# VectorE's selection of the second half of a slot's activations is placed behind the sum of snap and pz

## The chip, the cores and the metric

The kernel runs on one core of one Trainium2 chip. A core has five engines with an instruction stream each: TensorE (PE in the profile, with its weight loads as PEld), VectorE (DVE), ScalarE (ACT), GpSimd (POOL) and SyncE (SP). An engine works through its stream in order, and the engines wait for each other by semaphores. The metric is the device time of one execution in microseconds (us); the kernel before takes 1406.0 us (median of 3 runs, 1404.99 to 1407.55).

## The reference

Three stages follow each other, all in float32, on 8 batches of 512 tokens and 32 states:

```python
# attention both ways between x (8, 8, 512, 64) and state (8, 8, 32, 64)
a  = softmax(scale * x @ state.T);   xread = a @ state
a2 = softmax(scale * state @ x.T);   sread = a2 @ x
x = concat([xread, sread])           # 8 * (512 + 32) = 4352 tokens of 512
# first stage of products
x = ((x @ w_a) * (x @ w_b)) @ w_out          # w_a, w_b 512 x 1536
# second stage of products
h = x @ w_in                                  # w_in 512 x 2048
out = (h - tanh(h)) @ w_out2                  # w_out2 2048 x 512
```

The weights arrive as 64-bit numbers; the kernel decodes them on the chip.

## The kernel before

The attention and the first stage of products fill roughly the first half of the time. The second stage is what the change touches. Its work is cut into slots: 9 blocks of tokens (8 of 512, the last, the states, of 256) times 8 slots `j`. A slot computes two of the sixteen 128-row blocks of `h`, `h1` and `h2`, applies `h - tanh(h)` to them and multiplies by two 128-row pieces of the last weight matrix. A slot's own products are written by `pair_slot` (L777) as seven sums of 6 matmuls each of 128x256 (`part`, L690; a fixed 2x2 scheme with 7 products instead of 8), into three PSUM banks `py`, `px` and `pz`. Every float32 product is three matmuls of high and low halves. `px` is summed up over four parts and read in between: ScalarE copies it to `snap` (L787, L798, L813) and, the last time, into `h1` (L822). `pz` takes the parts T3 and T4: VectorE adds `snap` and `pz` into the right half of `h2` after T3 (L814, `at_v`) and into the left half after T4 (L830). T4 is added into the same bank that L814 reads, so T4 waits for L814. `h1` and `h2` have one buffer each.

The activation of the slot before runs meanwhile, in two halves g = 0 (on `h1`) and g = 1 (on `h2`), with work tiles u, t, y, k:

- ScalarE: u = h squared (L700), t = tanh h (L703), y = (u + c) squared (L711), k = relu(u - 0.49) (L715), which says where |h| is large.
- VectorE: `dve_yu` computes y (L719) and u (L720), `dve_rest` finishes the polynomial in y (L724), forms t = h - t (L725) and selects t into y where k is set (L726, the selection).
- ScalarE copies y to the high half of g (`g_hi`, L730), VectorE subtracts it for the low half (`g_lo`, L735).

`O(s, g, m)` (L747) multiplies g by the last weights into the accumulators `acc`: 6 matmuls of 128x256 for each of 4 accumulators `m`, of which the first two read the high half alone. In `pair_slot(s)` the O of slot s-2 with g = 1 and of slot s-1 with g = 0 stand between the parts. Of the 90 matmuls of a slot 42 are parts and 48 are O.

In steady state TensorE's order in a slot is: py 6, px 6, O 12 (s-2), px T2 6, pz T3 6, O 6, px T1 6, O 6 (the last of s-2) and O 6 (the first of s-1), px B22 6, O 6, pz T4 6, O 12.

The weights `wh` of a slot are loaded from DRAM by two DMAs (L272) into the buffers of slot s-2, the first with the pieces of the parts py, px, T2 and T3, the second with those of T1, B22 and T4.

What order an engine's stream has is decided when the program is built: a scheduler walks over the instructions with an estimate of their times and places what is ready first. `tc.issue_after(x)` adds an edge of order: what is written in its block comes behind x on x's engine. The edge has no semaphore of its own.

Of the kernel before, what the change touches and what calls it, by code (L numbers as in the profile page):

```python
# [12 lines left out]
ALU = mybir.AluOpType  # L13
# [32 lines left out]
def fused_kernel(ctx: ExitStack, tc, xT, xn, stp, stq, wA, wB, outT, outS):  # L46
    nc = tc.nc
# [592 lines left out]
    GG, HH, EW, RAWX = {}, {}, {}, {}  # L640
# [26 lines left out]
    def x_split(blk, i):  # L667
        b11, b12, b21, b22 = x_blocks(blk)
        if blk == NB:
            if i < 2:  # L670
                x_pair(blk, ("B11", "B21")[i], i, (b11, b21)[i])
        else:
            name, at, src = (("B11", 0, b11), ("B22", 2, b22), ("B21", 1, b21), ("T1", 3, b12), ("T2", 4, b22),
                             ("T3", 5, b11), ("T4", 6, b21))[i]
            x_pair(blk, name, at, src)

    def x_minus(blk, i):
        b11, b12, b21, b22 = x_blocks(blk)
        if blk < NB and i < 4:
            out, a, b = ((b12, b12, b11), (b22, b22, b12), (b21, b21, b22), (b11, b22, b11))[i]  # L680
            nc.vector.tensor_tensor(out, a, b, ALU.subtract)
# [5 lines left out]
    def part(dst, s, piece, x, first, last):  # L687
        for k in range(2):
            for i, (a, c) in enumerate(hi_lo):
                nc.tensor.matmul(dst, WP[s, piece][:, a, block(k)], XB[slots[s][0]][x][:, c, k, :],  # L690
                                 start=first and k == 0 and i == 0, stop=last and k == 1 and i == 2,
                                 skip_group_check=True)
# [5 lines left out]
    def act_u(s, g):  # L698
        ew_open(s, g)
        nc.scalar.activation(EW[s, g][0], HH[s][g], AF.Square)  # L700

    def act_t(s, g):
        nc.scalar.activation(EW[s, g][1], HH[s][g], AF.Tanh)  # L703

    def act_ut(s, g):
        act_u(s, g)
        act_t(s, g)

    def act_y(s, g):
        u, t, y, k = EW[s, g]  # L710
        return nc.scalar.activation(y, u, AF.Square, bias=consts[:, 0:1], scale=1.0)  # L711

    def act_k(s, g):
        u, t, y, k = EW[s, g]
        nc.scalar.activation(k, u, AF.Relu, bias=const2[:, 0:1], scale=1.0)  # L715

    def dve_yu(s, g):
        u, t, y, k = EW[s, g]
        nc.vector.scalar_tensor_tensor(y, y, PK, u, ALU.add, ALU.mult)  # L719
        nc.vector.scalar_tensor_tensor(u, t, C3, u, ALU.mult, ALU.mult)  # L720

    def dve_rest(s, g):
        u, t, y, k = EW[s, g]
        nc.vector.scalar_tensor_tensor(y, y, PC, u, ALU.add, ALU.mult)  # L724
        nc.vector.tensor_tensor(t, HH[s][g], t, ALU.subtract)  # L725
        nc.vector.copy_predicated(y, k.bitcast(I32), t)  # L726

    def g_hi(s, g):
        GG[s, g] = big.get([128, 2, 512], F32R, "g", MX + PHS + ["w21"])
        nc.scalar.copy(GG[s, g][:, 0, : width(s)], EW[s, g][2])  # L730

    def g_lo(s, g):
        n = width(s)
        gt = GG[s, g]
        return nc.vector.tensor_tensor(gt[:, 1, :n], EW.pop((s, g))[2], gt[:, 0, :n].bitcast(F32), ALU.subtract)  # L735

    def O(s, g, m):
        if not 0 <= s < len(slots):
            return
        (blk, j), n = slots[s], width(s)  # L740
        if j == 0 and g == 0:
            acc[m] = accp.tile([128, 512], F32, tag=f"acc{m}", name="acc")
        w, x = pair(WB[j + FP * g], block(m)), GG[s, g]
        cols = half[: n // 256]
        for i, (a, c) in enumerate(hi_lo):
            for h in cols:
                nc.tensor.matmul(acc[m][:, h], w[a], x[:, c, h], start=j + g + i == 0 and h is half[0],  # L747
                                 stop=j + g == FP and i == 2 and h is cols[-1], skip_group_check=True)

    def evac(s, g, m):  # L750
        if not 0 <= s < len(slots) or slots[s][1] < FP - 1 or g == 0:
            return
        (blk, j), n = slots[s], width(s)
        if m % 2 == 0:
            EV[0] = big.get([128, 2, 512], F32, "ev", RAW)
        e = EV[0][:, m % 2, :n]
        if m % 2 and blk == NB:
            nc.vector.tensor_copy(e, acc[m][:, :n])
        else:
            nc.scalar.copy(e, acc[m][:, :n])  # L760
        nc.sync.dma_start(outT[blk, m] if blk < NB else outS[m], e)
# [3 lines left out]
    def bank(i, name):  # L765

        pool = LAST[0] if i < 2 else abp
        return pool.tile([128, 512], F32, tag=f"p{i}", name=name)[:, half[0]]

    def OE(s, g, m):  # L770
        O(s, g, m)
        evac(s, g, m)

    def pair_slot(s):

        blk, j = slots[s]
        y_ = bank(0, "py")  # L777
        x_ = bank(1 + 2 * (s % 2), "px")
        sn = mix.get([128, 3, 256], F32, "snap", SQ)
        h1, h2 = (mix.get([128, 512], F32, "h", [nm]) for nm in (mix.names[2], "ml2"))  # L780
        part(y_, s, 2, "B21", True, True)
        part(x_, s, 1, "B11", True, True)
        yield
        if s:
            dve_rest(s - 1, 0)
            act_ut(s - 1, 1)
        first = nc.scalar.copy(sn[:, 0], x_)  # L787
        if s:
            with tc.issue_after(first.ins):
                act_y(s - 1, 1)  # L790
                act_k(s - 1, 1)
        OE(s - 2, 1, 0)
        OE(s - 2, 1, 1)
        if s:
            dve_yu(s - 1, 1)
        nc.vector.tensor_tensor(h1[:, half[0]], sn[:, 0], y_, ALU.add)
        part(x_, s, 3, "T2", False, True)
        second = nc.scalar.copy(sn[:, 1], x_)  # L798
        if s:
            with tc.issue_after(second.ins):  # L800
                g_hi(s - 1, 0)
            low = g_lo(s - 1, 0)
            with tc.issue_after(low.ins):
                dve_rest(s - 1, 1)
        z_ = bank(2 if s else 0, "pz")
        part(z_, s, 4, "T3", True, True)
        yield
        OE(s - 2, 1, 2)
        part(x_, s, 5, "T1", False, True)
        yield  # L810
        nxt = border.index(blk) + 1
        stage = j - 1 if j > 1 or blk == 0 else (0, None)[j]
        at_s = nc.scalar.copy(sn[:, 2], x_)  # L813
        at_v = nc.vector.tensor_tensor(h2[:, half[1]], sn[:, 2], z_, ALU.add)  # L814
        OE(s - 2, 1, 3)
        O(s - 1, 0, 0)
        follow = stage not in (None, -1) and nxt < len(border)
        if follow:
            with tc.issue_after(at_s.ins), tc.issue_after(at_v.ins):
                x_split(border[nxt], stage)  # L820
        part(x_, s, 6, "B22", False, True)
        whole = nc.scalar.copy(h1[:, half[1]], x_)  # L822
        if s:
            with tc.issue_after(whole.ins):
                g_hi(s - 1, 1)
            g_lo(s - 1, 1)
        yield
        O(s - 1, 0, 1)
        part(z_, s, 7, "T4", False, True)
        done = nc.vector.tensor_tensor(h2[:, half[0]], sn[:, 1], z_, ALU.add)  # L830
        if follow:
            with tc.issue_after(done.ins):
                x_minus(border[nxt], stage)
        O(s - 1, 0, 2)
        O(s - 1, 0, 3)
        HH[s] = h1, h2
        act_u(s, 0)
        squared = act_y(s, 0)
        with tc.issue_after(squared.ins):
            act_t(s, 0)  # L840
            act_k(s, 0)
        dve_yu(s, 0)
# [12 lines left out]
    def ew_between(s):  # L855
        dve_rest(s, 0)
        act_ut(s, 1)
        act_y(s, 1)
        act_k(s, 1)
        g_hi(s, 0)  # L860
        dve_yu(s, 1)
        g_lo(s, 0)
        dve_rest(s, 1)
        g_hi(s, 1)
        g_lo(s, 1)
# [60 lines left out]
    for blk in range(NB):  # L926
# [7 lines left out]
        for f in range(FA):  # L934
            v, t = stg[f] if stg else (None, None)
# [83 lines left out]
    first_pool.__exit__(None, None, None)  # L1019
    LAST.append(ctx.enter_context(tc.tile_pool(name="lastp", bufs=1, space=psum)))  # L1020
    slot = pair_slot(0)
    for f in range(FA):
        stages = {4: (0,), 5: (1, 2), 6: (3, 4), 7: (5, 6)}.get(f, ())
# [17 lines left out]
    for s, (blk, j) in enumerate(slots):  # L1041
        if s == 0:
            continue
        if j == 0 and blk < NB:
            xr_load(blk + 1)
        if blk < NB:
            for i, _ in enumerate(pair_slot(s)):
                if s == 1 and i == 0:
                    X1(NB, FA - 1)
        else:  # L1050
            plain_slot(s)
        if s < last - 1:
            wh_load(s + 2, slots[s + 2][1], nb=slots[s + 2][0] == NB)
# [53 lines left out]
```

## Time and profile before

| what | value |
|---|---|
| median of 3 runs | 1406.0 us (1404.99 to 1407.55) |
| the profiled execution, whole | 1407.53 us |
| its span, first to last instruction | 1405.7 us |
| PE busy | 1381.0 us, 98% |
| DVE busy | 1127.3 us, 80% |
| ACT busy | 896.3 us, 64% |
| granted TensorE clock, mean | 0.995 |
| second stage in pair slots | about 698 to 1349 us |

The page gives busy time by engine; the timeline gives single instructions, with start and duration, and runs of equal ones merged (xN). A matmul's duration in it overlaps the next one's, so the time that N matmuls take is read from start to start. On VectorE and ScalarE too the next instruction often starts before the end of the one before; what counts for a chain is again start to start, or end to start across engines. An idle time before an instruction stands in brackets with what ended it.

### The profile page before, as it was taken

The numbers are of one execution on the slowest core, as the hardware profiler recorded it, in microseconds if no ns is written. First come the engines' busy times: TensorE is split into PE (matmuls) and PEld (weight loads), VectorE is DVE, ScalarE is ACT, GpSimd is POOL, SyncE is SP. The second block draws the span as 40 slices with busy tenths as digits, with TensorE's granted clock in tenths as the row PEclk, the third lists the DMA queues.
The fourth block names the chain that finished last, engine by engine and source line by source line (L and its number), as shares of the span: only waits on it lengthen the run. The fifth ranks groups of instructions, "written<-read, shape, count | busy, mean of one in ns | idle before, by whom it ended". The sixth has DMA issues, their size and how long they took to land.

```text
span 1405.7 us, 26998 instructions
## 1 busy us (share of the span) xinstructions
PE 1381.0 (98%) x10464; PEld 1243.7 (88%) x10464; DVE 1127.3 (80%) x1972; ACT 896.3 (64%) x1740; POOL 207.4 (15%) x390
## 2 busy tenths in 40 slices
PE   6999999999999999999999999999999999999998
PEld 3667777888888888889999999999999999999998
DVE  7986657786644878772489999999999999998887
ACT  6765545564544556552467878778787877878675
POOL 0000001333111333321210111110111111011110
PEclk8999999999999999999999999999999999999999
DMA  9714457785546586855856757666675766667544
GB/s 382 262 53 148 135 159 233 222 270 163 159 130 194 177 263 217 257 180 170 292 181 201 227 169 231 188 215 210 201 227 168 232 187 218 210 188 221 168 148 132
DMA packets 103792, 280.69 MB, mean 200 GB/s; under 512 B 15216, under 2 KB 44400, under 8 KB 93936
## 3 DMA queue, kind: packets, MB, share of 16 engines
q0 software_dynamic: 41472, 178.28, 41.1%
q1 hardware_dynamic: 62192, 100.68, 22.0%
q8 instruction: 82, 1.34, 0.4%
q14 instruction: 46, 0.38, 0.1%
HBM read 216.53 MB, written 62.39 MB: 198 GB/s over the span
## 4 chain that ended last, share of the span: by engine, by line
PE 89%; DVE 6%; issue 2%; DMA 2%; ACT 1%; POOL 0%; SPq 0%; DVEq 0%; ACTq 0%; POOLq 0%
PE acc L747 26%; PE pab L464 19%; PE acc L464 17%; PE px L690 12%; PE pz L690 6%; PE py L690 3%; PE mq L555 2%; PE ph L851 1%; DMA raw<-in_wA 1%; PE sc L337 1%; DMA wh<-whd 1%; DVE mst L562 1%; DVE wa L133 0%; PE pr L412 0%; PE pt L349 0%
## 5 line engine op out<-in xcount | busy, mean ns | idle before, releaser
L747 PE MATMUL acc<-g,wo 128*128 128x256 f32 x3264 | 427.2, 277 | 0.3
L747 PEld LDWEIGHTS acc<-g,wo 128*128 128x128 f32 x3264 | 397.3, 188 | 1.0 <-DVE g L735 0.8
L464 PE MATMUL acc<-ph,wo 128*128 128x512 f32 (+1 forms) x1296 | 304.2, 380 | 0.0
L464 PE MATMUL pab<-hl,mx 128*128 128x512 f32 x1152 | 289.1, 397 | 2.3 <-DVE mst L562 2.2
L464 PEld LDWEIGHTS acc<-ph,wo 128*128 128x128 f32 x1296 | 230.6, 188 | 48.6 <-issue 3.7
L464 PEld LDWEIGHTS pab<-hl,mx 128*128 128x128 f32 x1152 | 211.3, 189 | 56.4 <-issue 6.8
L602 DVE TENSOR_TENSOR ac<-ac,pab 128x512 f32<-128x512 f32 (+1 forms) x108 | 70.7, 654 | 140.8 <-PE pab L464 140.5
L272 POOL DMA_DIRECT2D wh<-whd x144 | 77.6, 539 | 632.1 <-PE pz L690 581.9
L577 POOL DMA_DIRECT2D ml<-md x144 | 75.6, 527 | 402.8 <-DVE mx L583 235.9
L720 DVE SCALAR_TENSOR_TENSOR u<-t,u 128x512 f32<-128x512 f32 (+1 forms) x144 | 95.0, 660 | 23.2 <-ACT k L715 21.6
L599 ACT COPY ac<-pab 128x512 f32<-128x512 f32 (+1 forms) x108 | 60.5, 560 | 79.9 <-PE pab L464 79.7
L690 PE MATMUL pz<-T,wh 128*128 128x256 f32 x768 | 111.3, 281 | 0.0
L690 PE MATMUL px<-B,wh 128*128 128x256 f32 x768 | 108.7, 277 | 2.3 <-DMA wh<-whd 2.3
L726 DVE COPY_PREDICATED y<-k,t 128x512 f32<-128x512 int32 (+1 forms) x144 | 105.2, 730 | 4.7
L690 PE MATMUL px<-T,wh 128*128 128x256 f32 x768 | 108.2, 277 | 0.0
L735 DVE TENSOR_TENSOR g<-y,g 128x512 fp32r<-128x512 f32 (+1 forms) x144 | 95.1, 660 | 13.5 <-ACT g L730 10.1
L719 DVE SCALAR_TENSOR_TENSOR y<-y,u 128x512 f32<-128x512 f32 (+1 forms) x144 | 94.3, 655 | 10.6 <-ACT y L711 10.6
L711 ACT ACTIVATE y<-u,consts 128x512 f32<-128x512 f32 (+1 forms) x144 | 100.8, 700 | 2.7 <-DVE g L735 0.6
L690 PEld LDWEIGHTS px<-B,wh 128*128 128x128 f32 x768 | 96.9, 188 | 2.7 <-issue 2.5
L715 ACT ACTIVATE k<-u,const 128x512 f32<-128x512 f32 (+1 forms) x144 | 99.0, 687 | 0.0
L690 PEld LDWEIGHTS pz<-T,wh 128*128 128x128 f32 x768 | 97.7, 189 | 0.4 <-DVE h L814 0.2
L724 DVE SCALAR_TENSOR_TENSOR y<-y,u 128x512 f32<-128x512 f32 (+1 forms) x144 | 95.0, 660 | 2.5
(161 smaller groups left out, 2040.2 us busy)
## 6 DMA issues: line engine op xcount, KB each, us to landing
wh<-whd POOLq DMA_DIRECT2D x64, 1024.0 KB, 5.3
wh<-whd POOLq DMA_DIRECT2D x72, 768.0 KB, 4.8
ml<-md POOLq DMA_DIRECT2D x144, 128.0 KB, 2.8
raw<-in_wB SPq DMA_DIRECT2D x32, 512.0 KB, 4.6
whd<-hlb POOLq DMA_DIRECT2D x64, 256.0 KB, 3.1
rawab<-in_wA SPq DMA_DIRECT2D x12, 1024.0 KB, 9.4
md<-mst SPq DMA_DIRECT2D x48, 256.0 KB, 2.6
x1d<-ev SPq DMA_DIRECT2D x32, 256.0 KB, 3.3
```

Of the source, the lines that this page charges most:

```text
L272: nc.gpsimd.dma_start(t.rearrange("p a h c -> p a (h c)"), whd[j][:, a:b])
L464: nc.tensor.matmul(dst[:, cols], w[a], x[:, c, cols], start=first and i == 0, stop=last and i == 2)
L577: nc.gpsimd.dma_start(t[64 * G : 64 * G + 64, :], src[G, b])
L690: nc.tensor.matmul(dst, WP[s, piece][:, a, block(k)], XB[slots[s][0]][x][:, c, k, :], start=first and k == 0 and i == 0, stop=last and k = ...
L711: return nc.scalar.activation(y, u, AF.Square, bias=consts[:, 0:1], scale=1.0)
L715: nc.scalar.activation(k, u, AF.Relu, bias=const2[:, 0:1], scale=1.0)
L719: nc.vector.scalar_tensor_tensor(y, y, PK, u, ALU.add, ALU.mult)
L720: nc.vector.scalar_tensor_tensor(u, t, C3, u, ALU.mult, ALU.mult)
L724: nc.vector.scalar_tensor_tensor(y, y, PC, u, ALU.add, ALU.mult)
L726: nc.vector.copy_predicated(y, k.bitcast(I32), t)
L735: return nc.vector.tensor_tensor(gt[:, 1, :n], EW.pop((s, g))[2], gt[:, 0, :n].bitcast(F32), ALU.subtract)
L747: nc.tensor.matmul(acc[m][:, h], w[a], x[:, c, h], start=j + g + i == 0 and h is half[0], stop=j + g == FP and i == 2 and h is cols[-1], s ...
```

## The change

`dve_rest` is split into `dve_poly` (L724 and L725) and `dve_select` (L726). For the second half (g = 1) of the slot before, `pair_slot` calls `dve_poly` where `dve_rest` stood, and calls `dve_select` later, behind `at_v`, the sum of snap and pz, by an edge of order. The first half and the plain slots of the last block keep `dve_rest`.

```diff
     def dve_rest(s, g):
+        dve_poly(s, g)
+        dve_select(s, g)
+
+    def dve_poly(s, g):
         u, t, y, k = EW[s, g]
         nc.vector.scalar_tensor_tensor(y, y, PC, u, ALU.add, ALU.mult)
-        nc.vector.tensor_tensor(t, HH[s][g], t, ALU.subtract)
+        return nc.vector.tensor_tensor(t, HH[s][g], t, ALU.subtract)
+
+    def dve_select(s, g):
+        u, t, y, k = EW[s, g]
         nc.vector.copy_predicated(y, k.bitcast(I32), t)
...
             low = g_lo(s - 1, 0)
             with tc.issue_after(low.ins):
-                dve_rest(s - 1, 1)
+                dve_poly(s - 1, 1)
...
         at_v = nc.vector.tensor_tensor(h2[:, half[1]], sn[:, 2], z_, ALU.add)
+        if s:
+            with tc.issue_after(at_v.ins):
+                dve_select(s - 1, 1)
```

In the changed file the lines behind the edit have other numbers: L724 is L728, L725 is L729, the selection L726 is L733, `g_hi` L730 is L737, `g_lo` L735 is L742, O's L747 is L754, L796 is L803, the sum L814 is L821, and L830 is L840.

VectorE's order in a slot of the steady state before, from `g_lo` of g = 0 to the sum of the left half, with the semaphores that each instruction waits for (DVE_49 is VectorE's own, Activation_49 ScalarE's, PE_49 TensorE's):

```order
L735 TENSOR_TENSOR g<-y,g 128x512 [waits Activation_49]
L724 SCALAR_TENSOR_TENSOR y<-y,u 128x512 [waits DVE_49]
L725 TENSOR_TENSOR t<-h,t 128x512
L726 COPY_PREDICATED y<-k,t 128x512 [waits DVE_49]
L814 TENSOR_TENSOR h<-snap,pz 128x256 [waits Activation_49]
L662 TENSOR_TENSOR T_11408<-x1s,T_11408 128x512 [waits Activation_49]
L735 TENSOR_TENSOR g<-y,g 128x512 [waits Activation_49]
L830 TENSOR_TENSOR h<-snap,pz 128x256 [waits PE_49]
```

The same place of the changed kernel:

```order
L742 TENSOR_TENSOR g<-y,g 128x512 [waits Activation_49]
L728 SCALAR_TENSOR_TENSOR y<-y,u 128x512 [waits DVE_49]
L729 TENSOR_TENSOR t<-h,t 128x512
L821 TENSOR_TENSOR h<-snap,pz 128x256 [waits DVE_49,Activation_49]
L733 COPY_PREDICATED y<-k,t 128x512
L662 TENSOR_TENSOR T_11408<-x1s,T_11408 128x512 [waits Activation_49]
L742 TENSOR_TENSOR g<-y,g 128x512 [waits Activation_49]
L840 TENSOR_TENSOR h<-snap,pz 128x256 [waits PE_49]
```

The sum and the selection have changed places, and the wait for VectorE's own semaphore has gone from the selection to the sum: the sum writes `h2`, which the instruction ahead of it still reads (the slot before has the same buffer). An instruction that waits for two semaphores has one of the waits in an instruction of its own ahead of it, EVENT_SEMAPHORE in a trace. This place is the same in 61 of the 64 pair slots.

Where the slots begin, the scheduler also puts TensorE's work in another order. TensorE before, from the first O on; `wh_6992` are the second weights of slot 1, `wh_7261` and `wh_7263` those of slot 2, `wh_7414` the first of slot 3; `wo_0` and `wo_8` go with slot 0's two halves, `wo_1` with slot 1's first:

```order
L747 MATMUL acc<-g,wo_0_6615 128x256 x24
L690 MATMUL py<-B_6879,wh_7261 128x256 x4
L690 MATMUL px<-B_6825,wh_7414 128x256
L690 MATMUL pz<-T_6985,wh_6992 128x256 x6
L747 MATMUL acc<-g,wo_8_6673 128x256 x12
L690 MATMUL pz<-T_6982,wh_7261 128x256 x6
L747 MATMUL acc<-g,wo_8_6673 128x256
L690 MATMUL px<-T_6933,wh_7261 128x256 x6
```

And of the changed kernel:

```order
L754 MATMUL acc<-g,wo_0_6615 128x256 x24
L690 MATMUL pz<-T_6985,wh_6992 128x256 x6
L690 MATMUL py<-B_6879,wh_7261 128x256 x4
L754 MATMUL acc<-g,wo_8_6673 128x256 x4
L690 MATMUL pz<-T_6982,wh_7261 128x256 x4
L754 MATMUL acc<-g,wo_8_6673 128x256 x8
L690 MATMUL px<-T_6933,wh_7261 128x256 x6
L690 MATMUL pz<-T_6982,wh_7261 128x256 x2
```

T4 of slot 1 (`pz` with `wh_6992`) now stands ahead of the rest of slot 2's `py`, and the single matmul with slot 3's weights `wh_7414` has gone from there; it stands with the other five of its part, after slot 2's T4. From slot 4 on TensorE's order is the same as before. ScalarE's order differs in three places of slots 2 and 3 only, where `g_hi` comes one instruction later.

## Rows read from the trace of the kernel before

**Rows 1.** The page: busy us by engine (share of the span), instructions.
```profile
PE 1381.0 (98%) x10464; PEld 1243.7 (88%) x10464; DVE 1127.3 (80%) x1972; ACT 896.3 (64%) x1740; POOL 207.4 (15%) x390
```

**Rows 2.** Windows: stretch, length, busy (x) of PE, PEld, DVE, ACT, POOL, clock, DMA.
```profile
50.00:60.00 10.00, 9.03 (x68) 6.07 (x69) 9.97 (x18) 7.79 (x16) 0.00 (x0) 1.00 0.41 118
...
900.00:1000.00 100.00, 100.00 (x879) 99.98 (x878) 94.01 (x162) 74.84 (x148) 10.78 (x20) 1.00 0.64 199
```

**Rows 3.** Timeline of PE in the pair slots: start, duration, instruction, count.
```profile
749.00 1.52 PE L747 MATMUL acc<-g,wo 128*128 128x256 f32 x12
750.36 0.84 PE L690 MATMUL px<-B,wh 128*128 128x256 f32 x6
...
969.19 0.84 PE L690 MATMUL py<-B,wh 128*128 128x256 f32 x6
977.35 0.92 PE L690 MATMUL pz<-T,wh 128*128 128x256 f32 x6
...
979.51 0.84 PE L690 MATMUL py<-B,wh 128*128 128x256 f32 x6
```

**Rows 4.** Timeline of DVE in the slot that starts at 969.19.
```profile
970.01 0.69 DVE L720 SCALAR_TENSOR_TENSOR u<-t,u 128x512 f32<-128x512 f32 x1 [0.20 <-ACT k L715]
...
974.25 0.69 DVE L735 TENSOR_TENSOR g<-y,g 128x512 fp32r<-128x512 f32 x1
...
975.46 0.68 DVE L725 TENSOR_TENSOR t<-h,t 128x512 f32<-128x512 f32 x1
976.18 0.77 DVE L726 COPY_PREDICATED y<-k,t 128x512 f32<-128x512 int32 x1
976.82 0.41 DVE L814 TENSOR_TENSOR h<-snap,pz 128x256 f32<-128x256 f32 x1
977.15 0.69 DVE L662 TENSOR_TENSOR B<-x1s,B 128x512 fp32r<-128x512 f32 x1
```

**Rows 5.** Timeline of ACT around the same slot.
```profile
966.94 0.62 ACT L730 CAST g<-y 128x512 fp32r<-128x512 f32 x1
...
976.87 0.37 ACT L822 COPY h<-px 128x256 f32<-128x256 f32 x1 [1.15 <-PE px L690]
977.14 0.62 ACT L730 CAST g<-y 128x512 fp32r<-128x512 f32 x1
```

**Rows 6.** Timeline of DVE: L720 behind a wait in an instruction of its own.
```profile
733.41 0.68 DVE L719 SCALAR_TENSOR_TENSOR y<-y,u 128x512 f32<-128x512 f32 x1
734.20 0.69 DVE L720 SCALAR_TENSOR_TENSOR u<-t,u 128x512 f32<-128x512 f32 x1
```

**Rows 7.** Timelines of DVE and ACT: `g_hi` that waits for the selection.
```profile
707.55 0.76 DVE L726 COPY_PREDICATED y<-k,t 128x512 f32<-128x512 int32 x1
...
708.35 0.62 ACT L730 CAST g<-y 128x512 fp32r<-128x512 f32 x1 [0.30 <-DVE y L726]
```

**Rows 8.** Timeline of PE where the slots begin.
```profile
708.05 0.62 PE L690 MATMUL py<-B,wh 128*128 128x256 f32 x4
710.97 0.36 PE L690 MATMUL px<-B,wh 128*128 128x256 f32 x1 [2.29 <-DMA wh<-whd]
...
711.87 2.63 PE L747 MATMUL acc<-g,wo 128*128 128x256 f32 x12
...
723.70 1.53 PE L747 MATMUL acc<-g,wo 128*128 128x256 f32 x12
```

**Rows 9.** Timeline of PE: an idle time early in the kernel.
```profile
52.43 0.39 PE L491 MATMUL mp<-mx,minus 128*128 128x256 f32 x1 [0.97 <-ACT mx L490]
```

**Rows 10.** Timelines of PE and DVE at the end of the pair slots.
```profile
1344.12 1.52 PE L747 MATMUL acc<-g,wo 128*128 128x256 f32 x12
...
1354.45 3.36 PE L747 MATMUL acc<-g,wo 128*128 128x256 f32 x24
...
1349.70 0.69 DVE L720 SCALAR_TENSOR_TENSOR u<-t,u 128x512 f32<-128x512 f32 x1 [0.44 <-ACT k L715]
...
1354.21 0.69 DVE L735 TENSOR_TENSOR g<-y,g 128x512 fp32r<-128x512 f32 x1
```

## The prediction

> **What bounds the kernel now.** I began with the page [rows 1]: TensorE is busy for 98% of the span, VectorE for 80%. That is a mean over stages, so next the windows: in a stretch in the middle of the pair slots TensorE is busy for 100 us of 100, at granted clock 1.00, and VectorE for 94 [rows 2]. Two engines are near their limit there. A PE that reads 100% can still stop for tenths of a us, since its rows overlap; so the last view is the timeline, read from start to start. Twelve matmuls take 750.36 - 749.00 = 1.36 us, 0.1133 each [rows 3]. A slot has 90, so its floor is 10.20 us. The slot that starts at 969.19 takes 10.32, and the same work recurs at 749.00 and, 58 slots on, at 1344.12, on average (1344.12 - 749.00) / 58 = 10.26 per slot [rows 3, 10]. All that the pair slots lose is thus 0.06 each, 3.5 us in 58.
>
> The place of that loss is T4: its six matmuls at 977.35 read 0.92 instead of 0.84, with the sum L814 ending at 976.82 + 0.41 = 977.23 just ahead of them [rows 3, 4]. L814 stands behind the selection L726 on VectorE. The change takes the selection out of that path.
>
> The last question is what hangs on the selection. ScalarE's `g_hi` needs it (L730 starts 0.04 after the selection's end, 708.31 to 708.35, where it has waited [rows 7]), and behind `g_hi` ScalarE has u, y, t and k of the next half, on which VectorE's L720 waits [rows 4]. In the slot shown the selection ends at 976.18 + 0.77 = 976.95, while `g_hi` starts at 977.14, behind L822, which waits for TensorE [rows 4, 5]. So `g_hi` has 0.15 us to spare (0.19 less the 0.04). That is the cover of the selection's delay.
>
> **The change part by part.** No work is added on any compute engine. Per slot, two instructions change places and a wait moves.
>
> The sum. It no longer waits for the selection, so it is about 0.6 earlier and T4 never waits for it. What that gives alone is at most the 0.06 per slot above.
>
> The selection. Before, it starts 976.18 - 975.46 = 0.72 after the start of L725 [rows 4]. Now the sum stands between. The sum waits for L725's end too, because it writes the buffer of h2 that L725 reads, and that wait has an instruction of its own, since the sum also waits for ScalarE. The row for such a pair is L719, then L720 behind a separate wait: 734.20 - 733.41 = 0.79 [rows 6]. The nearest other price is the 0.72 of a wait inside the instruction. The low end is 0.60, the step from L735 two instructions on to L725 being 975.46 - 974.25 = 1.21 with no wait that binds [rows 4]. I take 0.79, as the same form on the same engine. From the sum to what follows it is 977.15 - 976.82 = 0.33. So the selection starts 0.79 + 0.33 = 1.12 after L725 instead of 0.72, 0.40 later, and the spare is 0.15.
>
> The Trainium skill, "VectorE: DVE Perf Modes", section "The DRAIN you can't avoid", says that between chained VectorE operations "the semaphore costs nothing extra", because the next operation waits for the pipe anyway. The rows here don't agree: 0.60 without a wait, 0.72 and 0.79 with one [rows 4, 6]. By the page the step would be 0.60; that is a rival below.
>
> So a new loop closes, from one slot to the next, without TensorE in it:
> - `g_hi` to L720, all ScalarE: 970.01 - 966.94 = 3.07 [rows 4, 5];
> - L720 to L725 of the second half, all VectorE in a row: 975.46 - 970.01 = 5.45 [rows 4];
> - L725 to the sum 0.79, the sum to the selection 0.33, the selection 0.77, to the next `g_hi` 0.04.
>
> Together 10.45 us. The same loop before is 3.07 + 5.45 + 0.72 + 0.77 + 0.04 = 10.05, below the floor of 10.20, and didn't show. 10.45 is above it by 0.25, and above what a slot takes now by 0.19. TensorE will stop where it needs g: at the third matmul of the first O with g = 0, which is the first that reads the low half. The low half is written at 974.25 + 0.69 = 974.94 in the slot at 969.19, and that matmul, the 57th of its slot, stands at 969.19 + 56 x 0.1133 = 975.54, 0.6 later; after two or three slots this slack is used and each slot costs 10.45. Behind L814, L662 and `g_lo` come later as well, but they have their slack with TensorE and aren't in the loop.
>
> The beginning of the slots. Before, TensorE stops for 2.29 us at 708.67 for slot 3's weights, which one matmul asks for too early, and then 12 matmuls take 2.63 instead of 1.52 [rows 3, 8], as at the lower of the two clock levels (1.2 and 2.4 GHz). From 708.05 to the O at 723.70 there are 100 matmuls, 11.33 us of work in 15.65: 4.32 lost. In the new order that matmul comes after slot 2's T4, and the loss goes. What is late next is g. I chained the new order by the same steps from 708.05: `g_hi` and `g_lo` of slot 0's second half end at 709.3 and 710.1, and TensorE, ready at 709.2, loses 0.8 there; for g of slot 1 it loses 0.3, since `g_hi` now stands behind a copy of px. The O that started at 723.70 starts at 720.4. In the next two slots both kernels lose a few tenths (TensorE for T4 before, for g now), and the first O of slot 5 that reads the low half, at 749.00 + 0.68 + 0.23 = 749.91 before, comes at 746.66: 3.25 gained. Bounds: 4.9 if nothing new waits, nothing if another early load takes the place of this one. The clock: the new stops are below 1 us each, and one of 0.97 early on left the granted clock at 1.00 in its window [rows 2, 9], so I count no slow stretch; one would cost the 1.1 of those 12 matmuls and as much again at most (4.32 less 2.29 is 2.03).
>
> The sum. From 746.66, 58 loops of 10.45 are 606.10, to 1352.76; the matmul that stands there now starts at 1344.12 + 0.68 + 0.23 = 1345.03 [rows 10]: 7.73 later, the early gain already in it. At the last slot before the plain ones the loop runs once more with 4.51 from L720 to `g_lo` (1349.70 to 1354.21 [rows 10]): 1.21 + 0.79 + 0.33 + 0.77 + 0.04 + 3.07 + 4.51 = 10.72, where before it is 9.92 (1345.03 to 1354.95, the 0.48 by which the 24 matmuls at 1354.45 exceed 2.88 counted in it): 0.8 more. The rest follows TensorE as before. In all +8.5 us on the profiled execution, whose span is 1405.7 and whole time 1407.53, 1.5 above the median; against the median of 1406.0 this is 1414.5.
>
> **The rivals.**
> 1. The loop binds, but at the lower price of a wait, 0.72: 0.07 less in 58 slots, 4.1 less, 1410.4. For it: the wait inside the instruction is what most rows show. Against: the built program has the separate wait.
> 2. The wait is hidden, 0.60, as the page has it. The loop is 10.26, just what a slot takes now; 58 times 0.19 and 0.2 at the end go, leaving the early gain: 1414.5 - 11.2 = 1403.3. Against it: every pair of dependent VectorE rows that I read shows the step.
> 3. Faster outright: the selection's delay is absorbed. The place is `g_hi`, where 0.15 is free, and TensorE's slack of 0.5; if ScalarE or VectorE made up 0.25 per slot, T4's stops would go and each slot take 10.20. 58 floors are 591.6, 3.5 less than now, and with the early gain 1399. It decides once the loop sums to 10.20 or less. For it: ScalarE idles 1.15 before L822 [rows 5]. Against: that idle lies beside the loop, and VectorE's 0.20 before L720 is a wait for the loop's own k.
> 4. The loop binds and the early gain fails (a new load in the way, or a fall of the clock at the new stops): up to 3.3 more, 1417.8.
>
> That the change does nothing isn't a case: the order of instructions shows it in 61 slots.
>
> **How the numbers follow.** The forecast, 1414.5, has 0.60 (its own range 1412 to 1417), rival 1 has 0.16, rival 2 has 0.09, rival 3 has 0.10, rival 4 has 0.05. 0.2%, 2.8 us, is about what a measurement of this kernel tells from no change. Forecast, 1 and 4 are slower by more: 0.81. Rival 2 lies at that bound and is split, 0.05 to same and 0.04 to faster; with rival 3 faster has 0.14. The range from 1409 to 1418 holds the forecast and rivals 1 and 4, 0.81; 2 and 3 are left out.
>
> **What would show it.** If right: L720 of the first half waits for k in every slot, slots of 10.4 to 10.5, and TensorE stops at the O of the slot before, on `g_lo`, no longer at T4; the step L725 to sum to selection reads 0.79 and 0.33; no wait for weights near 709 and a granted clock of 1.00 there. Wrong: slots of 10.26 or below, or `g_hi` still starting right behind L822.

## The result and the profile after

The changed kernel takes 1417.33 us (median of 5 runs, 1416.9 to 1417.46), the kernel before in the same comparison 1406.17 us (5 runs, 1404.99 to 1407.8): 1.0083 times the time, 95% interval [1.0072, 1.0094]. The forecast was 1414.5 us, slower. The profiled execution has a span of 1415.4 us and 1417.18 us in all, 9.7 us over the span before.

The page of the changed kernel: busy time as in [rows 1], then the share of the span on the chain that ended last.

```profile
PE 1390.9 (98%) x10464; PEld 1246.7 (88%) x10464; DVE 1128.8 (80%) x1972; ACT 903.4 (64%) x1740; POOL 208.0 (15%) x390
...
PE 45%; DVE 22%; issue 22%; ACT 8%; POOL 2%; DMA 1%; DVEq 0%; POOLq 0%; SPq 0%; ACTq 0%
```

The busy line says next to nothing: 98, 80 and 64% again, with the same counts. The chain does: TensorE has 45% of it now, VectorE 22% (before 89% and 6%). The waits from 740 to 1340 us say on what (total us, times, longest):

```profile
ACT g L737 <- DVE y L733: 28.1, 57, 0.9
DVE u L720 <- ACT k L715: 19.7, 58, 0.5
...
PEld px L690 <- ACT snap L805: 2.2, 7, 0.3
```

The first row is the new one. In 57 of the 58 slots of this stretch `g_hi` waits for the selection; before, the same view had no row for it. The second row stood there before too (19.8, 58).

VectorE in the slot that answers to [rows 4]:

```profile
971.67 0.69 DVE L720 SCALAR_TENSOR_TENSOR u<-t,u 128x512 f32<-128x512 f32 x1 [0.19 <-ACT k L715]
...
977.12 0.68 DVE L729 TENSOR_TENSOR t<-h,t 128x512 f32<-128x512 f32 x1
977.90 0.42 DVE L821 TENSOR_TENSOR h<-snap,pz 128x256 f32<-128x256 f32 x1
978.24 0.76 DVE L733 COPY_PREDICATED y<-k,t 128x512 f32<-128x512 int32 x1
...
982.12 0.69 DVE L720 SCALAR_TENSOR_TENSOR u<-t,u 128x512 f32<-128x512 f32 x1 [0.20 <-ACT k L715]
```

ScalarE in the same slot, to be read beside [rows 5]:

```profile
968.59 0.62 ACT L737 CAST g<-y 128x512 fp32r<-128x512 f32 x1 [0.45 <-DVE y L733]
...
972.59 0.35 ACT L794 COPY snap<-px 128x256 f32<-128x256 f32 x1
...
978.12 0.37 ACT L832 COPY h<-px 128x256 f32<-128x256 f32 x1 [1.18 <-PE px L690]
979.03 0.62 ACT L737 CAST g<-y 128x512 fp32r<-128x512 f32 x1 [0.54 <-DVE y L733]
```

L729 to the sum is 0.78, the sum to the selection 0.34, the loop from L720 to L720 982.12 - 971.67 = 10.45. `g_hi` no longer starts right behind the copy of px (976.87 and 977.14 in [rows 5]) but 0.91 later, behind the selection.

TensorE, from the start of the pair slots to their end (its rows of before are in [rows 3, 8, 10]):

```profile
709.15 0.62 PE L690 MATMUL py<-B,wh 128*128 128x256 f32 x4
...
720.41 1.52 PE L754 MATMUL acc<-g,wo 128*128 128x256 f32 x12
...
740.21 0.84 PE L690 MATMUL py<-B,wh 128*128 128x256 f32 x6
...
970.29 0.84 PE L690 MATMUL py<-B,wh 128*128 128x256 f32 x6
...
973.01 0.96 PE L690 MATMUL px<-T,wh 128*128 128x256 f32 x6
...
975.85 1.55 PE L754 MATMUL acc<-g,wo 128*128 128x256 f32 x12
...
1346.82 0.84 PE L690 MATMUL py<-B,wh 128*128 128x256 f32 x6
...
1363.91 2.86 PE L754 MATMUL acc<-g,wo 128*128 128x256 f32 x22 [0.73 <-DVE g L742]
```

Between the `py` at 740.21 and the one at 1346.82 lie 58 slots: 10.459 each on average. TensorE's own slots vary, from 10.20 to 10.91; VectorE's period, from one L720 of the first half to the next, doesn't: it is 10.42 to 10.50 in all of them but one (10.77). So the loop sets the pace, and TensorE follows it. The wait for weights near 709 is gone, and the O that stood at 723.70 stands at 720.41. TensorE's stop is visible at T2 (973.01, 0.96 instead of 0.84), hardly at the O (975.85, 0.03 over 1.52).

Every span below is taken apart in the same way, by the starts of `py`: "start" from slot 1 to slot 5, then 58 slots, then the rest from slot 63 to the end of the span. Slot 1 starts at 698.0 to 698.9 in all of them.

| kernel (one profiled execution each) | start | mean of 58 slots | rest |
|---|---|---|---|
| before | 45.41 | 10.261 | 67.06 |
| before, another execution | 43.37 | 10.256 | 67.02 |
| changed | 41.75 | 10.459 | 68.60 |
| new place in the first slots only | 42.26 | 10.250 | 67.11 |
| new place in the later slots only | 43.47 | 10.440 | 68.10 |
| changed, two buffers for h2 | 40.83 | 10.255 | 67.50 |
| changed, `g_hi` later | 42.21 | 10.219 | 67.59 |
| changed, both of these | 40.89 | 10.216 | 67.23 |
| changed, sum of py behind the selection | 42.58 | 10.341 | 67.72 |
| before, sum of py behind L814 | 44.59 | 10.228 | 67.04 |
| changed, first copy of px earlier | 41.75 | 10.418 | 68.23 |

### The profile page after: what moved, and what is told of

It reads as the page before. It is cut to its first block, busy times and chain, and to the rows that moved or that the text cites. A ratio compares the mean times of both kernels' runs of the same rounds, so it can differ in the third digit from the quotient of the medians.

```text
span 1415.4 us, 27063 instructions
## 1 busy us (share of the span) xinstructions
PE 1390.9 (98%) x10464; PEld 1246.7 (88%) x10464; DVE 1128.8 (80%) x1972; ACT 903.4 (64%) x1740; POOL 208.0 (15%) x390
## 4 chain that ended last, share of the span: by engine, by line
PE 45%; DVE 22%; issue 22%; ACT 8%; POOL 2%; DMA 1%; DVEq 0%; POOLq 0%; SPq 0%; ACTq 0%
PE pab L464 20%; PE acc L464 18%; DVE y L733 3%; DVE u L720 3%; DVE y L728 3%; DVE t L729 3%; POOL wh L272 2%; PE mq L555 2%; DVE g L742 2%; ACT y L711 2%; DVE y L719 2%; ACT g L737 2%; ACT k L715 1%; ACT u L700 1%; PE acc L754 1%
## 5 line engine op out<-in xcount | busy, mean ns | idle before, releaser
L754 PE MATMUL acc<-g,wo 128*128 128x256 f32 x3264 | 427.7, 277 | 1.1 <-DVE g L742 0.7
L754 PEld LDWEIGHTS acc<-g,wo 128*128 128x128 f32 x3264 | 396.8, 188 | 2.5 <-DVE g L742 1.7
L690 PE MATMUL px<-T,wh 128*128 128x256 f32 x768 | 115.3, 286 | 0.8
L737 ACT CAST g<-y 128x512 fp32r<-128x512 f32 (+1 forms) x144 | 86.3, 599 | 44.0 <-DVE y L733 39.4
L720 DVE SCALAR_TENSOR_TENSOR u<-t,u 128x512 f32<-128x512 f32 (+1 forms) x144 | 95.1, 660 | 23.9 <-ACT k L715 22.0
L742 DVE TENSOR_TENSOR g<-y,g 128x512 fp32r<-128x512 f32 (+1 forms) x144 | 95.1, 660 | 18.4 <-ACT g L737 12.6
L733 DVE COPY_PREDICATED y<-k,t 128x512 f32<-128x512 int32 (+1 forms) x144 | 104.9, 729 | 2.6
L690 PEld LDWEIGHTS px<-T,wh 128*128 128x128 f32 x768 | 97.5, 188 | 7.2 <-ACT snap L805 2.4
L719 DVE SCALAR_TENSOR_TENSOR y<-y,u 128x512 f32<-128x512 f32 (+1 forms) x144 | 94.3, 655 | 10.6 <-ACT y L711 10.6
```

## The experiments

All ratios are to the kernel before, run on the same chip between them.

**The change in a part of the slots.** The old place and the new one are chosen by the slot's number; the late one has `s > 4` for `s < 4`.

```diff
                 dve_poly(s - 1, 1)
+                if not (s < 4):
+                    dve_select(s - 1, 1)
...
-        if s:
+        if s and (s < 4):
             with tc.issue_after(at_v.ins):
                 dve_select(s - 1, 1)
```

> The new place of the selection in slots 1 to 3 alone, the old one from slot 4 on. Loop theory (the loss is a loop from ScalarE's g_hi over k, L720 and the sum to the selection and back, in every slot; the start gains): the start as in the changed kernel, where slot 5 began 3.3 us earlier, then slots alternating 10.20 and 10.33 as before: 1406.2 - 3.3 = 1402.9 (1402 to 1404). Rival 'start' (the new order where the slots begin costs, and the slots only carry it on): slower than before, over 1408.

Measured for the early part: 1404.69 us (11 runs), ratio 0.9992 [0.9984, 1.0001]. The loss goes, as the loop wants it, but the gain is 1.1 us and not 3, and the interval reaches to no change.

> The old place in slots 1 to 4, the new one from slot 5 on. Loop theory: the start as before, with its 2.3 us wait for slot 3's weights, then slots of 10.45 instead of 10.26: the loss of the changed kernel without its early gain, 1417.3 + 3.3 = 1420.6 (1419 to 1422). Rival 'start': about 1406.

Measured for the late part: 1417.19 us (5 runs), ratio 1.0077 [1.0064, 1.0091]. The steady slots alone bring all of the loss. But the kernel that has no early gain is as fast as the changed one (1417.33), where 3.4 us more were expected. Its TensorE shows part of why: it keeps the old order at the start and waits for slot 3's weights too.

```profile
711.06 0.36 PE L690 MATMUL px<-B,wh 128*128 128x256 f32 x1 [1.64 <-DMA wh<-whd]
...
711.94 1.52 PE L754 MATMUL acc<-g,wo 128*128 128x256 f32 x12
```

The wait is 1.64 instead of 2.29, and the 12 matmuls behind it take 1.52 and not 2.63 [rows 8].

**The kernel before once more.** So the next run was the kernel before itself, without any edit, for its start alone.

> The kernel before, unchanged, in another execution: how long TensorE stops near 709 us for slot 3's weights, and whether its clock falls. If the 4.3 us that were lost there in the profiled execution are usual, this one shows a wait of about 2.3 us and 12 matmuls of 2.6 again, the third slot 17.6 long. If they belong to that execution (the theory that fits the early gain of about 1 us measured with the new place in the first slots alone): a wait of 1.6 or less, 12 matmuls of 1.52, the third slot below 16.

Its one time is 1405.92 us, its span 1404.2. TensorE near 709:

```profile
708.83 0.63 PE L690 MATMUL py<-B,wh 128*128 128x256 f32 x4
711.00 0.36 PE L690 MATMUL px<-B,wh 128*128 128x256 f32 x1 [1.53 <-DMA wh<-whd]
...
711.88 1.52 PE L747 MATMUL acc<-g,wo 128*128 128x256 f32 x12
...
722.51 1.52 PE L747 MATMUL acc<-g,wo 128*128 128x256 f32 x12
```

From `py` to the O are 722.51 - 708.83 = 13.68 us, against 15.65 in [rows 8]. Of the 2.0 between them 0.8 are the longer wait, and that part isn't lost: TensorE came to it 0.8 earlier (708.05 for 708.83), while the weights landed at the same time (the matmul behind the wait starts at 710.97 and 711.00). The other 1.2 lie behind the wait: from the first of the 12 matmuls to the O are 723.70 - 711.87 = 11.83, here 722.51 - 711.88 = 10.63. The profile shown before the prediction had caught an execution in which the clock fell. Its windows (columns as in [rows 2]) show that directly:

```profile
712.00:714.00 2.00, 2.00 (x12) 2.00 (x11) 1.90 (x4) 1.47 (x4) 0.54 (x1) 0.51 0.34 43
714.00:716.00 2.00, 2.00 (x14) 2.00 (x13) 2.00 (x4) 1.17 (x2) 0.00 (x0) 0.64 0.84 292
```

The granted clock is 0.51 there, the lower of the two levels. In the other execution it is 1.00 from 700 to 720. The fall is 1.2 of the 1.6 us by which that execution's 1407.53 us exceeds this one's 1405.92.

**The wait opened on VectorE.** `h2` gets two buffers, so that the sum no longer writes what L729 of the slot before still reads.

```diff
-        GG[s, g] = big.get([128, 2, 512], F32R, "g", MX + PHS + ["w21"])
+        GG[s, g] = big.get([128, 2, 512], F32R, "g", MX + PHS)
...
-        h1, h2 = (mix.get([128, 512], F32, "h", [nm]) for nm in (mix.names[2], "ml2"))
+        h1 = mix.get([128, 512], F32, "h", [mix.names[2]])
+        h2 = w_tile(21, [128, 512], F32, "h") if s % 2 else mix.get([128, 512], F32, "h", ["ml2"])
```

> The changed kernel with two buffers for h2 in turn (one of the five g buffers given up for it), so that the sum no longer waits for the end of t = h - t. Loop theory: the step from L729 to the sum falls from 0.79 to 0.60 and the selection comes 0.93 after L729 instead of 1.12; the loop is 10.45 - 0.19 = 10.26, that is 11 us less in 58 slots: 1406 (1404 to 1408), with slots of 10.26 and k still waited for. Rival 'the separate wait costs nothing' (only that the sum stands in front costs): 0.60 is in it already, so no change, 1417. Rival 'g_hi not in it' (VectorE's T4 path bounds the slot): 1399, slots of 10.20.

Measured: 1403.61 us (11 runs), ratio 0.9983 [0.9974, 0.9992]. VectorE, with L729, the sum and the selection between two L720 of the first half:

```profile
966.48 0.69 DVE L720 SCALAR_TENSOR_TENSOR u<-t,u 128x512 f32<-128x512 f32 x1 [0.20 <-ACT k L715]
...
971.92 0.68 DVE L729 TENSOR_TENSOR t<-h,t 128x512 f32<-128x512 f32 x1
972.52 0.41 DVE L822 TENSOR_TENSOR h<-snap,pz 128x256 f32<-128x256 f32 x1
972.86 0.76 DVE L733 COPY_PREDICATED y<-k,t 128x512 f32<-128x512 int32 x1
...
976.73 0.69 DVE L720 SCALAR_TENSOR_TENSOR u<-t,u 128x512 f32<-128x512 f32 x1 [0.20 <-ACT k L715]
```

L822 is the sum in this kernel. The step is 0.60 without the wait, 0.78 with it, and 58 x 0.18 = 10.4 us hang on that. The mean slot is 10.255, as the loop's 10.26 wants. The loop still sets it: VectorE's L720 comes every 10.23 to 10.30 us, while TensorE takes its 10.20 in seven slots of eight and stops for the difference in the eighth, in which ScalarE copies the accumulators out (10.6 to 10.7). This is the strongest of the runs: from slot 4 on the order of TensorE, VectorE and ScalarE stays, only the reason to wait goes, and 13.7 us go with it (11.8 in the slots, 0.9 at the start, where the order differs, 1.1 in the rest). The time is 2.4 below the one expected, and 2.0 of that come from the start and the rest.

**The loop opened on ScalarE.** The wait stays, but `g_hi` and `g_lo` of the second half come behind u and y of the next one.

```diff
-        whole = nc.scalar.copy(h1[:, half[1]], x_)
-        if s:
-            with tc.issue_after(whole.ins):
-                g_hi(s - 1, 1)
-            g_lo(s - 1, 1)
+        nc.scalar.copy(h1[:, half[1]], x_)
...
         squared = act_y(s, 0)
+        if s:
+            with tc.issue_after(squared.ins):
+                g_hi(s - 1, 1)
+            g_lo(s - 1, 1)
```

> The changed kernel with g_hi and g_lo of the second half written behind y of the next first half, so that u and y on ScalarE no longer stand behind the selection. Loop theory: g_hi starts some 1.4 us later, the selection is done before that, and the loop is open: slots at TensorE's floor of 10.20, 58 x 0.06 below before, with the early gain 1406.2 - 3.5 - 3.3 = 1399.4 (1398 to 1402). Rival 'VectorE's own time' (VectorE is 93% busy, and the wait added there is what costs, whatever ScalarE does): about 1417. Rival 'a later g_hi makes TensorE wait for the second half of g': between, above 1406.

Measured: 1402.97 us (11 runs), ratio 0.9979 [0.997, 0.9988]. Slots are 10.219. ScalarE:

```profile
973.42 0.38 ACT L832 COPY h<-px 128x256 f32<-128x256 f32 x1 [1.15 <-PE px L690]
973.83 0.64 ACT L700 ACTIVATE u<-h 128x512 f32<-128x512 f32 x1
974.50 0.72 ACT L711 ACTIVATE y<-u,consts 128x512 f32<-128x512 f32 x1
975.13 0.60 ACT L737 CAST g<-y 128x512 fp32r<-128x512 f32 x1
```

u and y start without the selection, and this `g_hi` waits for nothing. (That of the first half now waits for its own selection, in 52 of 59 slots; it isn't in the loop.) VectorE's step is still 0.80 in this slot (L729 at 972.27, L821 at 973.07), so here the wait costs nothing; in the changed kernel it costs because it stands in a loop without slack. This run isn't as clean as the one before it: VectorE's order changes in the slots too, with `g_lo` later and y of the second half ahead of the first half's selection. The 1399.4 expected was missed by 3.6: of the early gain of 3.3 only 1.2 is there against the other execution of before (43.37 - 42.21), the slots stand 0.019 above the floor, 1.1 us in 58, and the rest is 0.6 longer than that of before.

**Both openings together.** The runs pointed to this version.

> The changed kernel with both openings of the loop: the high half's copy of the second half of g on ScalarE comes behind the square of the next half's activation (act_y), and h2 has two buffers (the odd slots take the one that g used). Nothing is left out. With either alone the kernel took 1403.0 and 1403.6. Loop theory: nothing of the loop is left above the floor, slots of 10.20, and the start is the better one of the run with two buffers of h2 (13.5, 10.25, 10.2 us for the first slots): about 1401.5 (1400 to 1403). Rival (what is left above 10.20 is not VectorE's chain): 1403 as with either alone.

Measured: 1401.11 us (5 runs), ratio 0.9964 [0.9951, 0.9978], the fastest of the study. Slots are 10.216: seven of eight at the floor of 10.20, the one in which ScalarE also copies the accumulators out at 10.31 to 10.38.

**One instruction less in the loop.** VectorE's sum of py into `h1` (L803), between y and u of the second half, goes behind the selection.

```diff
-        nc.vector.tensor_tensor(h1[:, half[0]], sn[:, 0], y_, ALU.add)
+        if not s:
+            nc.vector.tensor_tensor(h1[:, half[0]], sn[:, 0], y_, ALU.add)
...
+        if s:
+            with tc.issue_after(chosen.ins):
+                nc.vector.tensor_tensor(h1[:, half[0]], sn[:, 0], y_, ALU.add)
```

> The changed kernel, but VectorE's sum of py into h1 (L803), which stands inside the loop between y and u of a half, is placed behind the late selection. Nothing is left out. Loop theory: in this order u comes directly behind y and keeps a step of its own, so only 0.14 us of the loop's 10.45 go: slots of 10.31, 58 x 0.14 = 8.1 us less than the changed kernel's 1417.3, about 1409 (1406 to 1411). Rival (the slots are long for what the selection's place does to VectorE's load or to ScalarE's copies of px, whatever the loop's sum): slots stay at 10.4 to 10.5 and the time at 1416 to 1418.

Measured: 1410.13 us (6 runs), ratio 1.0029 [1.0018, 1.0041]. L720 to L720:

```profile
969.52 0.69 DVE L720 SCALAR_TENSOR_TENSOR u<-t,u 128x512 f32<-128x512 f32 x1
...
972.24 0.67 DVE L719 SCALAR_TENSOR_TENSOR y<-y,u 128x512 f32<-128x512 f32 x1
973.02 0.69 DVE L720 SCALAR_TENSOR_TENSOR u<-t,u 128x512 f32<-128x512 f32 x1
...
979.87 0.69 DVE L720 SCALAR_TENSOR_TENSOR u<-t,u 128x512 f32<-128x512 f32 x1
```

The loop is 10.35 and the mean slot 10.341. L719 to L720 is 0.78 now that they are neighbours, for 0.92 in the changed kernel with the sum between them (974.39 to 975.31), so of the 0.33 taken out 0.19 comes back as the wait of u for y. The slot follows the loop's sum to 0.03 us (10.31 expected).

**The same edit in the kernel before**, where the sum of py goes behind L814 instead.

> The kernel before, with the selection in its old place, but VectorE's sum of py into h1 is placed behind the sum of snap and pz (from the second slot on). Nothing is left out. In the kernel before TensorE loses 0.06 us per slot to T4, which waits for that sum. If that wait is what lengthens the slots from 10.20 to 10.26, a chain on VectorE that is 0.14 shorter takes it away: 58 x 0.06 = 3.5 us less than 1405.8, about 1402.3 (1401 to 1404). Rival (the 0.06 comes from elsewhere, as from px's copies on ScalarE): 1405 to 1407, slots of 10.26.

Measured: 1406.03 us (11 runs), ratio 0.9999 [0.999, 1.0008]: no change, a miss. Slots fall from 10.256 to 10.228, half of what was expected: T4 still stops in about one slot of four, one of them that in which ScalarE copies the accumulators out. And the start is 44.59 for 43.37, since TensorE's order changes there and it waits 2.14 us for the weights. 58 x 0.028 = 1.6 gained, 1.2 lost. The loss of 0.06 per slot is T4's all the same: summing what the steps from one matmul to the next have beyond 0.1133, from 745 to 1346, the other execution of before loses 3.2 us, 1.9 at T4 and 1.3 at the 12 matmuls of O right behind it, and this kernel 1.6, 1.4 and 0.2 at the same places. What was wrong is that a chain 0.14 shorter would take all of these stops away; it took away half of the loss.

**Where TensorE stops.** The changed kernel stops at T2, which waits for ScalarE's copy L794. Here that copy comes ahead of tanh.

```diff
-            act_ut(s - 1, 1)
+            act_u(s - 1, 1)
         first = nc.scalar.copy(sn[:, 0], x_)
         if s:
             with tc.issue_after(first.ins):
+                act_t(s - 1, 1)
                 act_y(s - 1, 1)
```

> The changed kernel, but ScalarE's first copy of px (L794), for which T2 waits in it, comes ahead of tanh of the second half instead of behind it. Nothing is left out. Tanh is then 0.25 us later, and VectorE needs it only some 2 us after that. Loop theory (the loop of g_hi, u, y, t, k, VectorE and the selection sets the slot, and the stop at T2 is only where TensorE meets it, since this copy stands behind the loop's k): the stop at T2 goes, TensorE stops elsewhere, at the first O with g = 0 (on g_lo) or at T1, slots stay at 10.45 and the time at 1416 to 1418. Rival (T2's wait for the copy is what the slots pay: 11.2 us in the changed kernel, 0.19 per slot): slots of 10.26 and 1405 to 1407.

Measured: 1414.69 us (5 runs), ratio 1.0066 [1.0052, 1.008]. Slots are 10.418, so 58 x 0.041 = 2.4 us less than in the changed kernel. TensorE:

```profile
763.27 0.84 PE L690 MATMUL px<-T,wh 128*128 128x256 f32 x6
...
765.99 1.79 PE L754 MATMUL acc<-g,wo 128*128 128x256 f32 x12
```

T2 takes its 0.84, and the O with the low half of g now takes 1.79 instead of 1.52. Taking all steps from one matmul to the next that are over 0.122 us, from 745 to 1346, and summing what they have beyond 0.1133, TensorE loses 11.5 us: 6.8 at the O and 4.3 at T2 and T1. In the changed kernel it was 12.3: 11.2 at T2 and T1, 0.8 at the O. The stop has moved and most of its size stayed: T2 is where the loop's lateness was met, not its cause. By the slots, (10.459 - 10.20) x 58 = 15.0 us over the floor have become 12.6, and the time is 1.3 below the range expected. The part that went lies in the slots in which ScalarE copies the accumulators out: VectorE's L720 to L720 is 10.15 to 10.22 in these seven, for 10.48 to 10.50 in the changed kernel, which is 2.1 of the 2.4 us, and some 10.45 in the others as before. Why it is shorter there stays open.

## Why the prediction was right, and where not

- The new loop (step: 10.45 per slot): right. Its terms measure 3.08, 5.45, 0.78, 0.34, 0.76 and 0.03, each within 0.01 of the forecast; the mean slot is 10.459, and over 58 slots that is 0.5 us more than forecast. Two openings at different places, on VectorE and on ScalarE (there with VectorE's order changed too), both bring the time below that of before; one instruction less shortens the slot to within 0.03 us of the loop's sum.
- The price of the wait (0.79, with 0.60 and 0.72 as bounds): right, 0.78, and 0.60 with the buffer doubled. Rival 1, the lower price, falls by the rows. Rival 2, the hidden wait, is what the run with two buffers shows when there is nothing to wait for; its forecast, 1403.3, is within 0.3 us of it. That closeness is luck: it took 11.2 off a forecast that was 2.8 low, and 13.7 went. The sentence of the Trainium skill, "VectorE: DVE Perf Modes", section "The DRAIN you can't avoid", that the semaphore costs nothing extra, measured there on eight copies in a row, does not agree with this pair of runs.
- Absorbed delay (rival 3): wrong here; neither ScalarE's idle time before L832 nor TensorE's slack was of use to the loop. It was of use only once `g_hi` was moved behind u and y.
- TensorE's stop "at the O, on `g_lo`": wrong. It was mostly at T2, on ScalarE's copy of px (11.2 of 12.3 us at T2 and T1, 0.8 at the O). The prediction carried g through the loop to TensorE, and missed that the copy of px stands behind k, u and t of the same late stretch of ScalarE (972.59, where `g_hi` starts at 968.59), with less slack than g. The size depended little on it, as the last run shows (12.6 of 15.0 us stayed).
- The early gain (3.25): the mis-sized term. Against the profiled execution of before it came true: slot 5 starts at 740.21 instead of 743.55. But 1.2 of it are a fall of the clock that the other execution of before doesn't have; and where TensorE came to the wait sooner, as it did by 0.8 in the profiled one, the wait was longer by as much. Against the other execution TensorE is 1.6 ahead at slot 5, counted from slot 1 (43.37 - 41.75). And even this is worth little: the kernel that has the new place only in the later slots is 1.7 behind the changed one at slot 5, 0.9 five slots later, 0.7 at slot 63 and 0.2 at the end of its span (717.12 and 716.96), all counted from slot 1. The first of these steps fits a loop that doesn't wait for TensorE; what made up the last 0.5, in the plain slots, stays open. Where TensorE does set the pace, with the new place in the first slots only, the start gains 1.1 (43.37 - 42.26), as much as the 1.1 measured, which is itself not clear of no change.
- From the profile to the median: the forecast was +8.5 on the profiled span and then took off 1.5 because that execution stood above the median. That was wrong, and it is the larger half of the 2.8 us by which the forecast was low: 1.2 of the excess were the same clock loss that the early gain already removed, so they were taken away twice. The sum itself was 1.2 low (9.7 measured): 0.5 in the loops, and 0.7 behind 1363.91 in the plain slots, in stops that I didn't trace. The step at the end, +0.8 at the last slot, came as worked out: 8.96 - (1346.82 - 1338.67) = 0.8, with 1338.67 the start of the same `py` before.
- Against the undisturbed execution of before the account closes: slots 606.61 - 594.82 = +11.8, rest +1.6, start -1.6, before slot 1 -0.5, together 11.3, with the medians 11.2 apart. The 0.5 before slot 1 isn't the change's, since the order of the instructions is the same up to there: slot 1 starts anywhere from 698.0 to 698.9 in these executions.

## What to carry to other kernels

Before moving an instruction, follow what it releases round to itself, over all engines but the busiest: a loop a quarter of a us longer than the bottleneck's own period costs that much in every round, and no busy share shows it. A stop of the bottleneck engine names the place where lateness is met; the loop is found at the engines whose waits point at each other. An early stall in one profiled execution is a sample: if a gain rests on it, compare that execution with the median first, and don't correct for the difference twice.

## What the runs showed of the hardware

- Of four waits for the same weights one brought TensorE's clock down. After 2.29 us it fell to 0.51 in one execution of the kernel before; after 1.53 in another, 1.64 with the new place in the later slots and 2.14 with the sum of py behind L814 it stayed at full speed: the 12 matmuls behind the wait took 1.52 each time. The wait that was followed by the fall is the longest of the four; whether its length decided it, these runs don't tell.
- The wait for the weights, in the same order of instructions, differs by 0.8 us between executions (1.53 and 2.29), not because the weights came later but because TensorE came to it 0.8 earlier: the matmul behind the wait starts at 711.00 and 710.97.
- On VectorE a wait on its own earlier instruction, in an instruction of its own, costs 0.18 us over the plain step (0.78 and 0.60, 128x512 in f32). Here that wait is only for the earlier one to have read a buffer, so a second buffer took it away.
